# Weights staged through one tile: where the rounding is done, how many groups are in flight, and which engine forms the sums of weight blocks

## The chip, the cores and the metric

The kernel runs on one core of one Trainium2 chip. The time is device microseconds (us) from launch to end; the profile's span is the time from the first to the last instruction of one profiled execution. The engines are TensorE (PE), VectorE (DVE), ScalarE (ACT), GpSimd (POOL) and SyncE (SP, which here only issues DMAs). GpSimd issues DMAs too. Each engine runs its own instructions strictly in the order in which they were built.

## The reference, cut to what matters

A two-step attention (8 batches, 8 heads, 576 rows, 32 pack rows) feeds a gated layer and then a second layer. The weights arrive as float64.

```python
def _attn_ref(q, k, v, p):
    ...
    p_packed = sm_attn(p, k, v)
    out = sm_attn(q, p_packed, p_packed)
    return out.astype(np.float32)

def _moe_ref(x, w_gate, w_val, w_out):
    gate = 1.0 / (1.0 + np.exp(-(x @ w_gate)))
    val = x @ w_val
    return (gate * val @ w_out).astype(np.float32)

def _moe2_ref(x, w_in, w_out):
    h = x @ w_in
    g = np.maximum(0.01 * h, h)
    return (g @ w_out).astype(np.float32)
```

Shapes: x is 4608 x 512; w_gate and w_val are 512 x 1536, w_out of the first layer 1536 x 512, w_in 512 x 2048, w_out of the second layer 2048 x 512.

## The kernel before, in words

The program has two parts. In the **gated part** the attention of batch b+1 and the gated products of batch b run side by side. Each batch has 12 gate steps: a step is two products on TensorE (L692), a sigmoid on ScalarE (L702, so there are 96 of them in all), a multiplication on VectorE (L708) and a store of the result to DRAM (`g1d`). In the **block part** six blocks of 768 tokens go through the remaining three products (L852, 5544 matrix multiplications) with a seven-product scheme for 2x2 blocks of matrices. It needs sums and differences of blocks of the weights and of the data.

Weights are float64 in DRAM, so each 128 x 512 piece is loaded as pairs of 32-bit words (`raw64`) and rounded to float32 by a **unit** of five instructions: `scale` and `low` on ScalarE, `shift` and `sign` on VectorE, and the integer addition `total` on GpSimd, which writes the result. In the kernel before, the first four work in tiles of their own, `cvs` and `cvf`, three of each. The first 24 units give the gating weights (tiles `wc`, which stay). The other 44 units belong to 22 **staged groups**, two units each, for the weights of the block part. A group has a tile `Y` of eight 256-column slots. Its two units fill four slots, `combine` fills the four others with sums and differences (four instructions, in two pairs), and then each half of `Y` (four slots and three) is split in a high and a low part: `high` on ScalarE (L317) casts it into a tile `HL`, `low` on GpSimd (L323) subtracts, and a DMA issued by GpSimd (L331) stores `HL` in DRAM (`wp`, `wu`, `wd`). There are two tiles `Y` and two tiles `HL`.

The order of instructions is made when the program is built, by a small planner. It walks through modelled time, gives each engine the ready task of lowest rank, and counts the tiles of each pool. Staged groups have rank 900 and more, behind everything in the gated part (`high` and `low` of a group are lifted to rank -1100). The costs that the planner assumes are formulas such as `gps(n)` for GpSimd; what it assumes for a DMA is its size plus 2.2 us.

Between the parts stand two markers. `opened_left` comes after all stored groups and all units: then the pool `stage` (raw64, cvs, cvf, Y, HL) gives its place to the tiles `rawg` and `wu` of the block part, so no load of the block part can start earlier. `opened_right` comes after the last gate step: then the pool of the attention gives its place to the operands `op`, so the block part's casts cannot start earlier.

```python
        opened_left = add("", 0, 0, open_left, sum([*stored.values(), *units], []))
        opened_right = add("", 0, 0, open_right, [glu_end[B - 1]])
```

Of the kernel before, what the change touches and what calls it, by code (L numbers as in the profile page):

```python
# [10 lines left out]
F32 = mybir.dt.float32  # L11
F32R = mybir.dt.float32r
I32 = mybir.dt.int32
U32 = mybir.dt.uint32
AF = mybir.ActivationFunctionType
ALU = mybir.AluOpType
AX = mybir.AxisListType
P = 128
# [11 lines left out]
class Plan:  # L30
# [15 lines left out]
    def add(self, engine, us, rank, fn, after=(), take=(), give=()):  # L46
        i = len(self.tasks)
        self.tasks.append((engine, us, rank, fn, [a for a in after if a is not None], take, give))
        for name in dict.fromkeys(name for name, _ in take):
            self.pools[name][1].append(i)  # L50
        for key in give:
            self.holders[key] = self.holders.get(key, 0) + 1
        return i
# [66 lines left out]
def act(n):  # L120
    return 0.13 + n * 0.00094


def dve(n):
    return 0.15 + n * 0.00105


def gps(n):
    return 0.05 + n * 0.0027
# [3 lines left out]
def pack_attention_glu_lrelu(  # L133
# [22 lines left out]
    nc = tc.nc  # L156
# [39 lines left out]
    stage = tc.alloc_tile_pool(name="stage", bufs=1, side="left")  # L196
# [7 lines left out]
    add = plan.add  # L204
# [6 lines left out]

    for name, n in (("raw64", 4), ("cv", 3), ("Y", 2), ("HL", 2)):
        plan.pool(name, n)

    def unit(key, rank, load, target, after=(), give=(), loads=1):

        t = {}

        def do_load():
            t["raw"] = stage.tile([P, 512, 2], I32, tag="raw64", bufs=4, name="raw64")
            load(t["raw"])

        def scale():
            t["s"] = stage.tile([P, 512], F32, tag="cvs", bufs=3, name="cvs")
            t["f"] = stage.tile([P, 512], I32, tag="cvf", bufs=3, name="cvf")
            nc.scalar.activation(t["s"], t["raw"][:, :, 1].bitcast(F32), AF.Copy, scale=2.0 ** -112)

        def low():  # L230
            nc.scalar.activation(t["f"], t["raw"][:, :, 0].bitcast(U32), AF.Copy, scale=2.0 ** -29)

        def shift():
            s = t["s"].bitcast(I32)
            nc.vector.tensor_single_scalar(s, s, 3, op=ALU.logical_shift_left)  # L235

        def sign():
            s = t["s"].bitcast(I32)
            nc.vector.scalar_tensor_tensor(  # L239
                out=s, in0=t["raw"][:, :, 1], scalar=-(1 << 31), in1=s,  # L240
                op0=ALU.bitwise_and, op1=ALU.bitwise_or,
            )

        def total():
            x = target().bitcast(I32)
            n = x.shape[1]
            nc.gpsimd.tensor_tensor(  # L247
                out=x,
                in0=t["s"].bitcast(I32).rearrange("p (a b) -> p a b", a=n),
                in1=t["f"].rearrange("p (a b) -> p a b", a=n),  # L250
                op=ALU.add,
            )

        L = add("DMA", 1.7, rank, do_load, after, take=[("raw64", ("raw64", key))])
        a = add("ACT", act(512), rank, scale, [L], take=[("cv", ("cv", key))])
        c = add("ACT", act(512), rank, low, [a], give=[("raw64", key)])
        s = add("DVE", 0.42, rank, shift, [a])
        s = add("DVE", 0.75, rank, sign, [s], give=[("raw64", key)])
        return add("POOL", gps(512), rank, total, [c, s, *after], give=[("cv", key), *give])

    def unit_gv(i, g, jh):
        w = (w_gate, w_val)[g]
# [17 lines left out]
    def staged(st, g, kk, rank):  # L280

        key, t = (st, g, kk), {}
# [17 lines left out]
        def target(half):  # L300
            def fn():
                if "y" not in t:
                    t["y"] = stage.tile([P, 8, 256], F32, tag="Y", bufs=2, name="Y")
                return t["y"][:, 0:2] if half else t["y"][:, 6:8]
            return fn

        def combine(*ops):
            def fn():
                y = t["y"]
                for o, a, b, op in ops:  # L310
                    nc.vector.tensor_tensor(out=y[:, o], in0=y[:, a], in1=y[:, b], op=op)  # L311
            return fn

        def high(x0, x1):
# [22 lines left out]
        y = ("Y", key)  # L337
        begin = add("", 0, rank, lambda: None, take=[("Y", y)])
        us = [unit((key, half), rank + 0.1 * half, load(half), target(half), [begin]) for half in range(2)]
        a1 = add("DVE", 2 * dve(256), rank, combine((2, 7, 1, ALU.add), (3, 2, 6, ALU.subtract)), us)  # L340
        a2 = add("DVE", 2 * dve(256), rank, combine((4, 6, 7, ALU.subtract), (5, 0, 3, ALU.subtract)), [a1])
        stored[key] = []
        for a, x0, x1 in ((a1, 0, 4), (a2, 4, 7)):
            n = (x1 - x0) * 256
# [414 lines left out]
    def block(n, opened_left, opened_right):  # L759
# [75 lines left out]
        def products(st, gm, gs, u, made, keep, finish):  # L835
# [3 lines left out]
            def key(*x):  # L839
                return (*x, n, st, gm)  # L840
# [35 lines left out]
            for i in ORDER:  # L876
                c = CHAIN[i]
                for g in gs:
                    wg = gm if st == "u" else g
                    L = load_weights(st, wg, i, u)  # L880
                    begin, end = g == gs[0], g == gs[-1]
                    task = add(
                        "PE", 2.07, u, mm(i, g, ("wu", n, st, wg, i), begin, end),
                        [L, made[i, g], *wait.get(i, [])],
                        take=[("acc", key("acc", c))] if begin and i in (1, 5, 6) else [],
# [155 lines left out]
    with tc.manual_schedule():  # L1041
# [11 lines left out]
        rank = 900.0  # L1053
# [39 lines left out]
```

## Time and profile before

| | us |
|---|---|
| median of 3 runs (1563.97 to 1570.9) | 1567.53 |
| time of the profiled execution | 1571.51 |
| its span | 1569.7 |
| PE busy in the span | 1426.4 |
| DVE busy in the span | 1082.0 |
| ACT busy in the span | 768.0 |
| POOL busy in the span | 437.7 |

The busy times are sums over the whole span. PE is busy for 91% of it. The profiled execution lies 4.0 us above the median, and its time 1.8 us above its span.

### The profile page before, as it was taken

What the parts mean: (1) busy time and instruction counts of PE and PEld (TensorE: products, weight loads), DVE (VectorE), ACT (ScalarE), POOL (GpSimd) and SP (SyncE); (2) the same over time, 40 slices, a digit from 0 to 9 for tenths busy, and PEclk for the clock granted to TensorE, in tenths of its full rate; (3) what the DMA queues carried; (4) which work ended last, traced back from release to release, by engine and by line L of the source; (5) the groups of instructions that cost most, each with busy time, mean ns of one, the idle gap of its engine ahead of it and who ended that gap; (6) DMA issues with size and microseconds to landing.
All of it is one profiled execution on the core that took longest, in us unless ns stands there. A gap on an engine that the chain in (4) does not pass through costs nothing.

```text
span 1569.7 us, 26707 instructions
## 1 busy us (share of the span) xinstructions
PE 1426.4 (91%) x10368; PEld 1336.0 (85%) x10368; DVE 1082.0 (69%) x1438; ACT 768.0 (49%) x1017; POOL 437.7 (28%) x514
## 2 busy tenths in 40 slices
PE   4687989998889828999999999999999999999995
PEld 1565777876768718999999999999999999999995
DVE  5787878967877627668566865687558755885491
ACT  4476666756565524454345433554355434543450
POOL 1332343314345652001710160026001620130006
PEclk8898999999999959999999999999999999999998
DMA  9994686776566879888998899889988898898884
GB/s 227 255 249 153 224 302 221 251 248 213 189 232 228 293 272 355 295 253 264 324 331 254 261 336 320 252 263 319 334 253 264 288 364 257 256 290 253 253 255 120
DMA packets 143070, 414.92 MB, mean 264 GB/s; under 512 B 24544, under 2 KB 35552, under 8 KB 142944
## 3 DMA queue, kind: packets, MB, share of 16 engines
q1 hardware_dynamic: 115744, 335.07, 67.3%
q0 software_dynamic: 27200, 78.14, 14.5%
q8 instruction: 83, 1.36, 0.4%
q14 instruction: 43, 0.35, 0.1%
HBM read 335.02 MB, written 78.12 MB: 263 GB/s over the span
## 4 chain that ended last, share of the span: by engine, by line
PE 70%; DMA 12%; DVE 7%; ACT 4%; POOL 3%; issue 3%; SPq 0%; POOLq 0%; ACTq 0%; DVEq 0%
PE ps_pair L852 60%; PE ps_pair L692 8%; DMA wd<-HL 2%; DMA raw<-in_moe_w_gate_dram 2%; DMA raw<-in_moe_w_out_dram 2%; DMA wu<-HL 1%; DVE Y L311 1%; DMA v<-in_v_dram 1%; POOL out_dram L1027 1%; POOL HL L323 1%; DVE ml L676 1%; DMA rawg<-g1d 1%; PE ps_pair L659 1%; POOL Y L247 1%; DVE cvs L235 1%
## 5 line engine op out<-in xcount | busy, mean ns | idle before, releaser
L852 PE MATMUL ps_pair<-op,wu 128*128 128x384 f32 x5544 | 965.7, 337 | 39.5 <-DMA wu<-wp 33.5
L852 PEld LDWEIGHTS ps_pair<-op,wu 128*128 128x128 f32 x5544 | 963.6, 189 | 41.5 <-ACT op L795 33.5
L1027 POOL DMA_DIRECT2D out_dram<-os x256 | 150.3, 595 | 618.8 <-DVE os L1014 609.5
L795 ACT CAST op<-rawg 128x768 fp32r<-128x768 f32 x168 | 138.3, 835 | 245.3 <-DVE rawg L786 121.3
L692 PE MATMUL ps_pair<-Ah,ml 128*128 128x288 f32 x768 | 181.1, 318 | 52.8 <-DVE ml L676 22.5
L800 DVE TENSOR_TENSOR op<-rawg,op 128x768 fp32r<-128x768 f32 x168 | 158.3, 951 | 87.3 <-ACT op L795 86.1
L692 PEld LDWEIGHTS ps_pair<-Ah,ml 128*128 128x128 f32 x768 | 126.9, 197 | 101.9 <-ACT sg L702 27.6
L869 DVE TENSOR_TENSOR tmp<-ps_pair,tmp 128x768 f32<-128x768 f32 x72 | 68.8, 956 | 154.4 <-PE ps_pair L852 106.0
L692 PE MATMUL ps_pair<-Al,mh 128*128 128x288 f32 x768 | 169.9, 303 | 0.3 <-DVE Al L581 0.2
L692 PE MATMUL ps_pair<-Ah,mh 128*128 128x288 f32 x768 | 169.0, 302 | 0.0
L795 ACT CAST op<-G 128x768 fp32r<-128x768 f32 x168 | 134.7, 834 | 59.8 <-PE ps_pair L852 44.8
L800 DVE TENSOR_TENSOR op<-G,op 128x768 fp32r<-128x768 f32 x168 | 155.7, 948 | 7.7 <-ACT op L795 7.3
L323 POOL TENSOR_TENSOR HL<-Y,HL 128x1024 fp32r<-128x1024 f32 (+1 forms) x44 | 94.7, 2155 | 129.7 <-ACT HL L317 128.3
L692 PEld LDWEIGHTS ps_pair<-Al,mh 128*128 128x128 f32 x768 | 128.6, 196 | 0.9 <-DVE Al L581 0.9
L692 PEld LDWEIGHTS ps_pair<-Ah,mh 128*128 128x128 f32 x768 | 127.8, 195 | 0.0
L925 POOL DMA_DIRECT2D rawg<-g1d x96 | 68.0, 712 | 160.7 <-ACT op L795 66.6
L988 ACT ACTIVATE G<-G 128x768 f32<-128x768 f32 x96 | 81.2, 846 | 59.0 <-DVE G L985 58.0
L247 POOL TENSOR_TENSOR Y<-cvs,cvf 128x512 int32<-128x512 int32 x44 | 58.5, 1334 | 149.2 <-DVE cvs L239 104.8
L863 ACT COPY tmp<-ps_pair 128x768 f32<-128x768 f32 x72 | 57.5, 799 | 84.5 <-PE ps_pair L852 84.0
L786 DVE TENSOR_TENSOR rawg<-rawg 128x768 f32<-128x768 f32 x96 | 90.2, 952 | 4.1 <-DMA rawg<-g1d 3.3
L786 DVE TENSOR_TENSOR G<-G 128x768 f32<-128x768 f32 x96 | 91.1, 950 | 0.3
L708 DVE TENSOR_TENSOR sg<-sg,ps_pair 128x576 f32<-128x576 f32 x96 | 71.5, 744 | 28.0 <-ACT sg L702 11.2
(75 smaller groups left out, 1147.3 us busy)
## 6 DMA issues: line engine op xcount, KB each, us to landing
wu<-wu SPq DMA_DIRECT2D x168, 512.0 KB, 4.6
wu<-wd SPq DMA_DIRECT2D x168, 512.0 KB, 4.5
wu<-wp SPq DMA_DIRECT2D x126, 512.0 KB, 5.0
g1d<-sg SPq DMA_DIRECT2D x96, 288.0 KB, 4.0
rawg<-g1d POOLq DMA_DIRECT2D x48, 384.0 KB, 8.7
raw<-in_moe_w_out_dram SPq DMA_DIRECT2D x28, 512.0 KB, 6.8
raw<-in_k_dram SPq DMA_DIRECT2D x16, 576.0 KB, 5.1
raw<-in_q_dram SPq DMA_DIRECT2D x16, 576.0 KB, 6.2
```

What stands on the lines that cost most here:

```text
L247: nc.gpsimd.tensor_tensor(out=x, in0=t["s"].bitcast(I32).rearrange("p (a b) -> p a b", a=n), in1=t["f"].rearrange("p (a b) -> p a b", a=n) ...
L323: nc.gpsimd.tensor_tensor(out=hl[:, :, 1], in0=t["y"][:, x0:x1], in1=hl[:, :, 0].bitcast(F32), op=ALU.subtract,)
L692: nc.tensor.matmul(ps[:, t, :HS], w, x[:, t * HS:(t + 1) * HS], start=(n == 0), stop=(n == len(pairs) - 1),)
L708: nc.vector.tensor_tensor(out=sg, in0=sg, in1=st["gv", f, 1][:, :, :HS], op=ALU.mult)
L786: nc.vector.tensor_tensor(out=src(g, o), in0=src(g, a), in1=src(g, b), op=ALU.subtract)
L795: nc.scalar.copy(h, src(g, c))
L800: (nc.gpsimd if on_pool(i, g) else nc.vector).tensor_tensor(out=l, in0=src(g, c), in1=tiles["op", st, i, g][0].bitcast(F32), op=ALU.subtract)
L852: nc.tensor.matmul(ps[c][:, m, :TB], a, x[:, kk, :], start=(fresh and kk == 0 and y == 0), stop=(end and kk == 1 and y == 2), skip_group_c ...
L869: nc.vector.tensor_tensor(out=T[x], in0=ps[c][:, :, :TB], in1=T[y], op=ALU.add)
L925: nc.gpsimd.dma_start(out=t[:, :, t0 - base:t0 - base + m], in_=g1d[b][:, f:f + 2, s0:s0 + m])
L988: nc.scalar.activation(dest(), dest(), AF.Prelu, alpha=0.01)
L1027: nc.gpsimd.dma_start(out=ob[:, s0:s0 + m, d0:d0 + 32], in_=tiles["os", c][32 * y:32 * y + 32, x, t0:t0 + m],)
```

## The change: what it does

1. `scale` writes its float32 result into the tile of the result at once (`wc` or a slot pair of `Y`); `shift`, `sign` and `total` work there in place. The tile `cvs` is gone; the pool `cv` counts only `cvf` and is taken at `low`. So it is now `scale` that waits for a free `Y`, and the load of `raw64` no longer does. Into `wc`, the rows written are two runs of 256 columns instead of one of 512.
2. There are three tiles `Y` instead of two.
3. The four sums and differences of a group go from VectorE to GpSimd (88 instructions of 128 x 256 in all).
4. The planner is told new costs: 0.6 and 0.78 us for `shift` and `sign`, and GpSimd's formula for the sums.

```diff
-    for name, n in (("raw64", 4), ("cv", 3), ("Y", 2), ("HL", 2)):
+    for name, n in (("raw64", 4), ("cv", 3), ("Y", 3), ("HL", 2)):
...
         def scale():
-            t["s"] = stage.tile([P, 512], F32, tag="cvs", bufs=3, name="cvs")
-            t["f"] = stage.tile([P, 512], I32, tag="cvf", bufs=3, name="cvf")
-            nc.scalar.activation(t["s"], t["raw"][:, :, 1].bitcast(F32), AF.Copy, scale=2.0 ** -112)
+            x = t["x"] = target()
+            nc.scalar.activation(
+                x, t["raw"][:, :, 1].bitcast(F32).rearrange("p (a b) -> p a b", a=x.shape[1]),
+                AF.Copy, scale=2.0 ** -112,
+            )
...
         def total():
-            x = target().bitcast(I32)
-            n = x.shape[1]
+            x = t["x"].bitcast(I32)
             nc.gpsimd.tensor_tensor(
-                out=x,
-                in0=t["s"].bitcast(I32).rearrange("p (a b) -> p a b", a=n),
-                in1=t["f"].rearrange("p (a b) -> p a b", a=n),
-                op=ALU.add,
+                out=x, in0=x, in1=t["f"].rearrange("p (a b) -> p a b", a=x.shape[1]), op=ALU.add
             )
 
-        L = add("DMA", 1.7, rank, do_load, after, take=[("raw64", ("raw64", key))])
-        a = add("ACT", act(512), rank, scale, [L], take=[("cv", ("cv", key))])
-        c = add("ACT", act(512), rank, low, [a], give=[("raw64", key)])
-        s = add("DVE", 0.42, rank, shift, [a])
-        s = add("DVE", 0.75, rank, sign, [s], give=[("raw64", key)])
-        return add("POOL", gps(512), rank, total, [c, s, *after], give=[("cv", key), *give])
+        L = add("DMA", 1.7, rank, do_load, take=[("raw64", ("raw64", key))])
+        a = add("ACT", act(512), rank, scale, [L, *after])
+        c = add("ACT", act(512), rank, low, [a], take=[("cv", ("cv", key))], give=[("raw64", key)])
+        s = add("DVE", 0.6, rank, shift, [a])
+        s = add("DVE", 0.78, rank, sign, [s], give=[("raw64", key)])
+        return add("POOL", gps(512), rank, total, [c, s], give=[("cv", key), *give])
...
-                    t["y"] = stage.tile([P, 8, 256], F32, tag="Y", bufs=2, name="Y")
+                    t["y"] = stage.tile([P, 8, 256], F32, tag="Y", bufs=3, name="Y")
...
-                    nc.vector.tensor_tensor(out=y[:, o], in0=y[:, a], in1=y[:, b], op=op)
+                    nc.gpsimd.tensor_tensor(out=y[:, o], in0=y[:, a], in1=y[:, b], op=op)
...
-        a1 = add("DVE", 2 * dve(256), rank, combine((2, 7, 1, ALU.add), (3, 2, 6, ALU.subtract)), us)
-        a2 = add("DVE", 2 * dve(256), rank, combine((4, 6, 7, ALU.subtract), (5, 0, 3, ALU.subtract)), [a1])
+        a1 = add("POOL", 2 * gps(256), rank, combine((2, 7, 1, ALU.add), (3, 2, 6, ALU.subtract)), us)
+        a2 = add("POOL", 2 * gps(256), rank, combine((4, 6, 7, ALU.subtract), (5, 0, 3, ALU.subtract)), [a1])
```

How the planner now orders the instructions shows at three places. The changed file is shorter by one line there, so L317 of before is L316 of the changed kernel, L702 is L701, L795 is L794, L713 is L712.

**ScalarE, end of the gated part.** `sg` rows are the sigmoids of gate steps, `HL` rows the casts of the staged groups, `cvs` and `cvf` rows belong to units, and `op` rows are the first casts of the block part. Before:

```order
L702 ACTIVATE sg<-ps_pair 128x576 x2
L317 CAST HL<-Y 128x4x256
L317 CAST HL<-Y 128x3x256
L228 ACTIVATE cvs<-raw_6287 128x512
L231 ACTIVATE cvf<-raw_6287 128x512
L228 ACTIVATE cvs<-raw_6298 128x512
L231 ACTIVATE cvf<-raw_6298 128x512
L317 CAST HL<-Y 128x4x256
L317 CAST HL<-Y 128x3x256
L795 CAST op<-rawg 128x768 x11
```

Changed, at the last cast into `HL`:

```order
L701 ACTIVATE sg<-ps_pair 128x576
L316 CAST HL<-Y 128x3x256
L672 CAST mh<-ps_pair 128x1024
L316 CAST HL<-Y 128x4x256
L701 ACTIVATE sg<-ps_pair 128x576
L316 CAST HL<-Y 128x3x256
```

Changed, at the end of the gated part:

```order
L701 ACTIVATE sg<-ps_pair 128x576 x2
L672 CAST mh<-ps_pair 128x1024
L701 ACTIVATE sg<-ps_pair 128x576 x3
L794 CAST op<-rawg 128x768 x5
L862 COPY tmp<-ps_pair 128x768
L794 CAST op<-rawg 128x768 x4
```

Before, two groups end behind the last sigmoid (the 96th); in the changed order the last cast of the last group stands behind the 78th, and nothing of the staging stands between the last sigmoid and the block part. Of the 44 casts into `HL`, those that stand behind fewer than 12 sigmoids, 12 to 23, 24 to 35 and so on are 0, 5, 5, 6, 4, 6, 7, 7 and 4 (behind the 96th) before, and 2, 6, 10, 4, 8, 8, 6, 0 and 0 in the changed order.

**GpSimd, the last staged group.** `Y<-cvs,cvf` and `Y<-Y,cvf` are `total`, `HL<-Y,HL` is `low`, `Y<-Y` the sums, `wd_75` the store, and `rawg` the first loads of the block part. Before:

```order
L331 DMA wd_75<-HL 128x4x512
L247 TENSOR_TENSOR Y<-cvs,cvf 128x512
L331 DMA wd_75<-HL 128x3x512
L247 TENSOR_TENSOR Y<-cvs,cvf 128x512
L323 TENSOR_TENSOR HL<-Y,HL 128x4x256
L323 TENSOR_TENSOR HL<-Y,HL 128x3x256
L331 DMA wd_75<-HL 128x4x512
L331 DMA wd_75<-HL 128x3x512
L925 DMA rawg<-g1d_57 128x2x384 x3
```

Changed:

```order
L322 TENSOR_TENSOR HL<-Y,HL 128x4x256
L249 TENSOR_TENSOR Y<-Y,cvf 128x512
L330 DMA wd_75<-HL 128x4x512
L310 TENSOR_TENSOR Y<-Y 128x256 x2
L322 TENSOR_TENSOR HL<-Y,HL 128x3x256
L310 TENSOR_TENSOR Y<-Y 128x256 x2
L330 DMA wd_75<-HL 128x3x512
L322 TENSOR_TENSOR HL<-Y,HL 128x4x256
L330 DMA wd_75<-HL 128x4x512
L322 TENSOR_TENSOR HL<-Y,HL 128x3x256
L330 DMA wd_75<-HL 128x3x512
L924 DMA rawg<-g1d_57 128x2x384 x3
```

The sums now stand in GpSimd's own queue, in pairs, between the additions, the subtractions and the stores of neighbouring groups.

**SyncE, the first loads of staged weights.** `wu` rows are those loads, `g1d_63` and `g1d_64` rows the stores of gate steps of the last two batches, `raw` rows the loads of float64 pieces. Before:

```order
L713 DMA g1d_64<-sg 128x576 x3
L288 DMA raw_6287<-in_moe_w_out_dram 128x1024
L713 DMA g1d_64<-sg 128x576
L288 DMA raw_6298<-in_moe_w_out_dram 128x1024
L767 DMA wu<-wp_65 128x1024
L767 DMA wu<-wp_66 128x1024
```

Changed:

```order
L712 DMA g1d_62<-sg 128x576 x2
L712 DMA g1d_63<-sg 128x576 x10
L766 DMA wu<-wp_65 128x1024
L712 DMA g1d_63<-sg 128x576
L766 DMA wu<-wp_66 128x1024
L712 DMA g1d_63<-sg 128x576
L766 DMA wu<-wp_67 128x1024
```

The first loads of staged weights moved from behind the last load of a float64 piece to a place among the last stores of batch 6, a batch earlier; all six that there is room for stand ahead of the last ten stores of the last batch.

## Rows read from the trace of the kernel before

**Rows 1.** The page: span, and the chain that ended last, by engine.

```profile
span 1569.7 us, 26707 instructions
...
PE 70%; DMA 12%; DVE 7%; ACT 4%; POOL 3%; issue 3%; SPq 0%; POOLq 0%; ACTq 0%; DVEq 0%
```

**Rows 2.** Busy time by stretch: between the parts, and block part (us and instructions).

```profile
546.91:613.29 66.38, 27.30 (x145) 26.28 (x145) 34.27 (x41) 25.05 (x33) 30.01 (x33) 0.74 0.82 298
613.29:1543.78 930.49, 930.10 (x5354) 929.34 (x5355) 622.73 (x697) 409.45 (x509) 183.31 (x298) 1.00 0.88 286
```

**Rows 3.** Timeline, 546 to 581 us: start, duration, engine, what [idle before].

```profile
546.48 0.43 PE L692 MATMUL ps_pair<-Ah,mh 128*128 128x288 f32 x2
...
547.01 0.75 DVE L708 TENSOR_TENSOR sg<-sg,ps_pair 128x576 f32<-128x576 f32 x1 [0.30 <-issue]
...
565.42 1.53 POOL L331 DMA_DIRECT2D wd<-HL  x2
572.69 5.65 POOL L925 DMA_DIRECT2D rawg<-g1d  x8 [5.74 <-issue]
...
579.28 0.83 ACT L795 CAST op<-rawg 128x768 fp32r<-128x768 f32 x1 [16.77 <-DMA rawg<-g1d]
...
580.14 0.96 DVE L800 TENSOR_TENSOR op<-rawg,op 128x768 fp32r<-128x768 f32 x1 [19.30 <-ACT op L795]
...
580.16 0.69 PE L852 MATMUL ps_pair<-op,wu 128*128 128x384 f32 x1 [33.25 <-DMA wu<-wp]
```

**Rows 4.** Busy time between every twelfth sigmoid: PE, PEld, DVE, ACT, POOL, clock, DMA.

```profile
122.76:189.05 66.29, 55.53 (x587) 46.04 (x587) 55.17 (x94) 40.42 (x56) 17.06 (x12) 0.92 0.63 209
189.05:251.81 62.76, 56.68 (x592) 45.98 (x593) 50.73 (x81) 39.23 (x57) 25.03 (x18) 0.92 0.75 253
251.81:310.33 58.52, 57.26 (x677) 46.50 (x677) 52.24 (x96) 42.88 (x61) 24.32 (x17) 1.00 0.71 237
310.33:367.38 57.05, 52.53 (x533) 43.12 (x532) 43.70 (x68) 30.73 (x44) 17.61 (x13) 0.97 0.66 211
367.38:432.26 64.88, 57.34 (x611) 47.19 (x618) 51.95 (x82) 40.06 (x57) 24.17 (x18) 0.95 0.69 226
432.26:500.58 68.32, 61.22 (x655) 50.91 (x654) 48.35 (x81) 43.21 (x60) 29.69 (x22) 0.95 0.65 227
500.58:545.36 44.78, 40.76 (x320) 35.20 (x320) 32.04 (x45) 25.54 (x38) 30.01 (x23) 0.96 0.81 289
sum 422.60, PE 381.32 PEld 314.94 DVE 334.18 ACT 262.06 POOL 167.90; mean PE 54.47 PEld 44.99 DVE 47.74 ACT 37.44 POOL 23.99
```

**Rows 5.** Instructions of four lines: duration in ns, least, median and most.

```profile
L311 DVE TENSOR_TENSOR Y<-Y x88: 381/424/2610, 132.1 to 560.4; 128x256 f32<-128x256 f32 x88
...
L235 DVE TENSOR_SCALAR cvs<-cvs x68: 378/421/1619, 11.9 to 555.7; 128x512 int32<-128x512 int32 x68
...
L247 POOL TENSOR_TENSOR Y<-cvs,cvf x44: 1264/1288/1625, 106.0 to 558.0; 128x512 int32<-128x512 int32 x44
```

**Rows 6.** What ScalarE waited for ahead of L317: us in all, times.

```profile
  DVE Y L311: 31.0, 17
```

**Rows 7.** Timeline of GpSimd, first and last of five first halves in the tail.

```profile
496.70 2.40 POOL L323 TENSOR_TENSOR HL<-Y,HL 128x1024 fp32r<-128x1024 f32 x1 [4.69 <-ACT HL L317]
...
547.56 2.33 POOL L323 TENSOR_TENSOR HL<-Y,HL 128x1024 fp32r<-128x1024 f32 x1 [1.74 <-ACT HL L317]
552.96 1.82 POOL L323 TENSOR_TENSOR HL<-Y,HL 128x768 fp32r<-128x768 f32 x1 [3.07 <-ACT HL L317]
```

**Rows 8.** Timeline of GpSimd and VectorE around 189 us, side by side.

```profile
189.22 2.38 POOL L323 TENSOR_TENSOR HL<-Y,HL 128x1024 fp32r<-128x1024 f32 x1 [1.94 <-ACT HL L317]
...
189.73 2.48 DVE L311 TENSOR_TENSOR Y<-Y 128x256 f32<-128x256 f32 x2
```

**Rows 9.** Groups of instructions: busy us, mean ns of one, and idle before.

```profile
L311 DVE TENSOR_TENSOR Y<-Y 128x256 f32<-128x256 f32 x88 | 56.0, 666 | 9.5 <-POOL Y L247 8.6
...
L235 DVE TENSOR_SCALAR cvs<-cvs 128x512 int32<-128x512 int32 x68 | 42.8, 639 | 27.8 <-ACT cvs L228 27.7
```

More of the change, by code (lines that the diff above doesn't have):

```diff
@@ L225, in scale, with low @@
         def scale():
-            t["s"] = stage.tile([P, 512], F32, tag="cvs", bufs=3, name="cvs")
+            x = t["x"] = target()
[3 more added lines that the diff above has]
+            )
+        def low():
             t["f"] = stage.tile([P, 512], I32, tag="cvf", bufs=3, name="cvf")
-            nc.scalar.activation(t["s"], t["raw"][:, :, 1].bitcast(F32), AF.Copy, scale=2.0 ** -112)
@@ L230, in low @@
-        def low():
             nc.scalar.activation(t["f"], t["raw"][:, :, 0].bitcast(U32), AF.Copy, scale=2.0 ** -29)
         def shift():
-            s = t["s"].bitcast(I32)
-            nc.vector.tensor_single_scalar(s, s, 3, op=ALU.logical_shift_left)
+            x = t["x"].bitcast(I32)
+            nc.vector.tensor_single_scalar(x, x, 3, op=ALU.logical_shift_left)
         def sign():
-            s = t["s"].bitcast(I32)
+            x = t["x"].bitcast(I32)
             nc.vector.scalar_tensor_tensor(
-                out=s, in0=t["raw"][:, :, 1], scalar=-(1 << 31), in1=s,
-                op0=ALU.bitwise_and, op1=ALU.bitwise_or,
+                out=x, in0=t["raw"][:, :, 1].rearrange("p (a b) -> p a b", a=x.shape[1]),
+                scalar=-(1 << 31), in1=x, op0=ALU.bitwise_and, op1=ALU.bitwise_or,
@@ L242, in sign @@
             )
         def total():
-            x = target().bitcast(I32)
-            n = x.shape[1]
+            x = t["x"].bitcast(I32)
             nc.gpsimd.tensor_tensor(
-                out=x,
-                in0=t["s"].bitcast(I32).rearrange("p (a b) -> p a b", a=n),
-                in1=t["f"].rearrange("p (a b) -> p a b", a=n),
-                op=ALU.add,
-            )
-        L = add("DMA", 1.7, rank, do_load, after, take=[("raw64", ("raw64", key))])
-        a = add("ACT", act(512), rank, scale, [L], take=[("cv", ("cv", key))])
```

## The prediction

> **What bounds the kernel now.** I read the chain that ended last first: TensorE has 70% of it, and the rest is DMA, VectorE and ScalarE work that must lie where TensorE waits [rows 1]. So the second view is busy time by stretch. In the block part TensorE is busy for 930.10 of 930.49 us at full clock [rows 2]; nothing that the change touches is in that stretch, and it can become neither shorter nor longer. Between the last gated matrix multiplication, which ends at 546.91 us, and 613.29 us TensorE does only 27.30 us of work, at a granted clock of 0.74 [rows 2, 3]. The reader should see there that this hole isn't the price of changing parts as such. The timeline names its cause: the last multiplication of a gate step ends at 547.8 us, but GpSimd issues the last two stores of staged weights from 565.42 us on, the first load of the block part goes out at 572.69 us, and ScalarE's first cast waits for it until 579.28 us [rows 3]. The last staged groups are late, not the gated part.
>
> How large is the hole in terms of the block part? In 930.10 us it runs 5354 recorded multiplications, 0.1737 us each; the 145 that lie before 613.29 us would need 25 us [rows 2]. So the block part runs as if it had started, undisturbed, at 613.3 - 25.0 = 588.3 us. From 546.9 us that makes 41.4 us lost.
>
> The gated part is the third view, cut at every twelfth sigmoid [rows 4]. Over seven such stretches TensorE is busy for 381.3 of 422.6 us: 41.3 us are idle, spread thin. VectorE is busy for 50 us of an average 63 in the first six, GpSimd for 23.
>
> **The change, part by part.**
>
> *Moving the staging ahead.* By the order of the changed kernel the last cast of the last group stands behind the 78th sigmoid, where two groups stood behind the 96th. Engines are in order, so the staging must be over about 18 gate steps before the gated part is. A gate step took 44.78/12 = 3.7 us where no attention ran beside it [rows 4], so the six loads of staged weights and those of `rawg` have more than 50 us where they now have none. What is left of the hole is the hand-over that needs the last gate step: its multiplication ends 0.9 us after TensorE, one cast of 0.83 us and one subtraction of 0.96 us follow [rows 3], together about 3 us. Then comes a start-up, in which casts, subtractions and differences of the first operands must keep ahead of TensorE. In the run of before TensorE lost 33.1 - 25.0 = 8.1 us between 580.16 and 613.29 us, with the loads late as well [rows 2, 3]. With the loads done, the start-up is between nothing and 8 us; I take 4, the middle. Gain: 41.4 - 3 - 4 = 34 us.
>
> *The sums on GpSimd.* The trace has no floating-point addition of 256 columns on GpSimd. The nearest rows are its additions of 512 columns, 1.288 us in the median [rows 5], and subtractions of 1024 and 768 columns, 2.40 and 1.82 us [rows 7]. The last two give 2.27 ns for a column and so 0.66 us for 256; half of 1.288 is 0.64, and going down from 1.288 by 2.27 ns a column gives 0.71. I take 0.70 us, 2.8 us for a group and 62 us for all 88. GpSimd's work for a group becomes 2 x 1.29 + 2.8 + 2.40 + 1.82 + two DMA issues of 0.77 (1.53 for two [rows 3]) = 11.1 us. VectorE is rid of 56.0 us [rows 9]; only 88 x 0.424 = 37 us of these are the work itself [rows 5], the rest is waiting, to which I come.
>
> *How fast can a group be staged?* In the tail, where nothing but two tiles `HL` holds the staging, four periods take 547.56 - 496.70 = 50.9 us, 12.7 us a group [rows 7]. If the sums take 2.8 us there for VectorE's 4 x 0.424 = 1.7, the period is 13.8 us; if all of the 2.8 us came on top, 15.5. Between the tenth and the 78th sigmoid there are 68 steps, and at the 63 us that twelve steps take [rows 4] that is 357 us. Twenty-two groups need 304 us at 13.8 and 341 at 15.5. So it fits on the whole, but not everywhere: ten casts, five groups, stand in the 24th to 35th step, and 5 x 13.8 = 69 us is 6 more than the 62.8 us that this stretch took [rows 4]. The stretches with four groups need 55 us of 57.1 and 64.9, which fits. At 15.5 us a group the same count gives 15 + 5 = 20 us. Since a cast that waits holds up the sigmoids behind it in ScalarE's queue, this lengthens the gated part, by 6 us as I take it (the sums replace VectorE's rather than come on top), by 20 at most.
>
> *What is gained beside it.* ScalarE waited 31.0 us, 17 times, for VectorE's sums [rows 6]; those waits now depend on GpSimd instead. If they and VectorE's relief gave back a third of the 41.3 us of idle time in the gated part, it would be 15 us shorter. I take nothing of it, because the casts still wait for sums and stores, and keep 15 as the bound.
>
> *Rounding in place, and the third tile.* `scale`, `low`, `sign` and `total` keep their element counts; ScalarE, VectorE and GpSimd write as much as before. `shift` could take longer where its rows are two runs: a median of 0.421 us now [rows 5], and if it cost the 0.639 that it has on average [rows 9], 68 x 0.22 = 15 us of VectorE's time lie beside a VectorE that the sums leave with 37 us less. At no cost on the path; the cover is VectorE's idle 13 us in each stretch of 63 [rows 4].
>
> *Sum.* The profiled execution took 1571.5 us. Less 34, plus 6: 1543.5. It lies 4.0 us above the median of the runs, so against the median the same sum is 1567.5 - 28 = 1539.5. I say 1539.
>
> **What speaks against it: the port of GpSimd and VectorE.** An instruction of VectorE on two operands in SBUF can be held up by GpSimd: at 189.22 us GpSimd starts a subtraction of 2.38 us, and two sums that VectorE starts at 189.73 take 2.48 us for two where the median is 0.42 each [rows 5, 8]. The worst single sum took 2610 ns [rows 5]. In the mean a sum lost 0.666 - 0.424 = 0.24 us and a shift 0.22 [rows 5, 9], while GpSimd was busy for a third of the time. The sums leave VectorE, and with them this loss of 21 us, but GpSimd will be busy about twice as much, and shifts, signs and the softmax's subtractions and products stay on VectorE: some twenty in a stretch of 63 us (four in each of three or four groups, six of the attention). At twice the loss, 0.45 us each, that is 9 us of a VectorE which had 13 idle and lost 8 of work: no term.
>
> The Trainium skill, in "SBUF — State Buffer", section "Who interferes with whom", has this as an exclusive lock: a VectorE instruction with two SBUF inputs and a GpSimd instruction that reads SBUF exclude each other, and whichever is second is blocked for the whole of the other. By that rule a held-up instruction waits for what is left of an addition or subtraction, half of 1.3 to 2.4 us on average; the rows at 189 us agree with it. The sum would be the same by either, but the rule bears out the slower rival below, in which the waits are long ones.
>
> **The rivals.**
> 1. *GpSimd becomes the bound of the staging* and its waits move into the gated part: the period is 15.5 us, the gated part 20 us longer, 1567.5 - 34 + 20 = 1553.5. For it: 11.1 us of 12.7 are GpSimd's own work. Against it: the planner spaced the casts with GpSimd at 1.43 us for an addition that takes 1.29 (its formula, 0.05 + 512 x 0.0027), so it left GpSimd room.
> 2. *The gated part gets shorter too*, by 15 us, with VectorE relieved: 1567.5 - 34 - 15 = 1518.5. For it: VectorE is the busiest engine there after TensorE. Against it: TensorE's idle pieces are short and stretches with few groups idle no less.
> 3. *VectorE waits for GpSimd at every two-operand instruction* (the other side). Without the sums of three groups (12 x 0.666 us = 8) VectorE needs about 42 us of 63; twenty instructions that wait w each add 20w. It becomes the bound at w = 1.0 us, and at w = 1.3 six stretches longer by 5 us each, 30 in all, eat the gain of 28: from there on the kernel is slower. At w = 1.5 it takes 1567.5 - 34 + 6 x 9 = 1587. Against it: w is 0.22 now.
> 4. *The hole stays in another shape*: the block part's first operands wait for a load or for space that is freed as late as before, and the 34 us shrink to what the gated part loses. 1567. Against it: both markers and all loads stand earlier in the order; only `opened_right` hangs on the last gate step.
>
> **How the numbers follow.** My forecast gets 0.52, rival 1 0.18, rival 2 0.14, rival 3 0.08, rival 4 0.08. The likeliest case's own range is 1528 to 1550 (6 us either way for the stretch of ten casts, 4 for the start-up). The range runs from rival 2 to past rival 1, 1518 to 1560; rivals 3 and 4 lie outside. A measurement of this kernel can tell about 0.5%, 8 us. Forecast, rival 1 and rival 2 are all faster by more: 0.84. Rival 4 is the same, 0.08; rival 3 slower, 0.08.
>
> **What the changed profile should show.** The last store of staged weights is issued some 60 us before the last gated multiplication; the first cast into `op` begins within 2 us of the last multiplication of a gate step, and TensorE's wait at the change of parts is about 3 us, not 33. The block part's 930 us stand. A sum on GpSimd takes 0.65 to 0.75 us and GpSimd is busy for some 62 us more. The stretch from the 24th to the 36th sigmoid is the one that grows. I am wrong if the last gated multiplication ends later than 567 us (rival 1 and beyond), if shifts take over 1 us in the median (rival 3), or if the first operands wait for DMA (rival 4).

## The result and the profile after

The changed kernel takes 1539.96 us in the median of four runs (1537.68 to 1542.83), the kernel before beside it 1568.99. The ratio is 0.9822 with a 95% interval of 0.9802 to 0.9842 (the quotient of these two medians alone would be 0.9815). The forecast was 1539 us.

The page, span and the chain that ended last:

```profile
span 1535.9 us, 26671 instructions
...
PE 78%; DMA 8%; DVE 5%; ACT 4%; issue 2%; POOL 2%; SPq 1%; POOLq 0%; ACTq 0%; DVEq 0%
```

TensorE's share of the chain went from 70% to 78% [rows 1]. The second view is busy time by stretch: from the end of the gated part to 615 us, and on to the last sum but one of the block part, which began at 1543.78 us in the kernel before. The columns are those of [rows 2].

```profile
549.39:615.00 65.61, 61.06 (x337) 60.28 (x337) 46.50 (x53) 28.48 (x37) 8.66 (x12) 0.95 0.79 277
615.00:1509.96 894.96, 894.96 (x5164) 894.70 (x5163) 602.09 (x674) 399.89 (x497) 178.67 (x290) 1.00 0.87 284
```

Before, 66.4 us behind the gated part held 27.3 us of TensorE's work [rows 2]; now 65.6 us hold 61.1. From the end of the gated part to that sum it was 66.4 + 930.5 = 996.9 us, and it is 960.6: the hole gave 36.3 us. The gated part itself ends 2.5 us later (549.4 us for 546.9). 36.3 - 2.5 = 33.8 is the whole difference of the two spans. The medians differ by 29.0 only: the profiled execution of before lies 2.5 us above its median here, that of the changed kernel 2.3 below. So no sum of terms from this one pair is good to better than 5 us.

The timeline around the change of parts, GpSimd first, then VectorE, ScalarE and TensorE:

```profile
484.95 0.77 POOL L330 DMA_DIRECT2D wd<-HL  x1 [0.30 <-POOL HL L322]
489.70 7.20 POOL L924 DMA_DIRECT2D rawg<-g1d  x10 [3.98 <-DMA wd<-HL]
...
549.48 0.76 DVE L707 TENSOR_TENSOR sg<-sg,ps_pair 128x576 f32<-128x576 f32 x1 [2.42 <-PE ps_pair L691]
...
552.50 3.76 ACT L794 CAST op<-rawg 128x768 fp32r<-128x768 f32 x5 [4.01 <-DMA g1d<-sg]
...
553.39 0.69 PE L851 MATMUL ps_pair<-op,wu 128*128 128x384 f32 x1 [4.00 <-ACT op L794]
```

The last staged store is issued 64 us ahead of the last gated multiplication, the loads of the block part follow 4 us later, when that store has landed, and TensorE waits 4.00 us instead of 33.25 [rows 3]. What is left isn't only cast and subtraction: the first cast waits until the last gate step's store has landed (`DMA g1d<-sg`), 2.3 us after that step's multiplication on VectorE, because `op` takes over the memory of the pool that holds `sg`.

The gated part, cut at every twelfth sigmoid:

```profile
124.22:194.03 69.81, 54.44 (x583) 44.94 (x591) 57.53 (x92) 45.43 (x64) 38.56 (x34) 0.90 0.80 262
194.03:257.39 63.36, 57.09 (x659) 46.49 (x666) 51.44 (x74) 42.02 (x58) 50.96 (x44) 0.97 0.85 280
257.39:321.50 64.11, 57.70 (x638) 47.64 (x619) 53.62 (x88) 46.95 (x70) 32.41 (x28) 0.97 0.82 265
...
444.38:503.66 59.28, 55.10 (x605) 44.72 (x604) 42.68 (x61) 35.35 (x48) 48.47 (x50) 0.97 0.67 238
503.66:547.84 44.18, 44.18 (x370) 39.16 (x369) 16.08 (x19) 12.88 (x18) 0.28 (x1) 1.00 0.50 189
sum 423.62, PE 377.84 PEld 313.91 DVE 324.55 ACT 264.10 POOL 257.21; mean PE 53.98 PEld 44.84 DVE 46.36 ACT 37.73 POOL 36.74
```

GpSimd's work in these stretches rose from 167.9 to 257.2 us, and the whole is 1 us longer [rows 4]. The last stretch has no staging and no idle TensorE.

The lines that answer to the sums and shifts of before (duration in ns: least, median, most):

```profile
L310 POOL TENSOR_TENSOR Y<-Y x88: 720/742/1293, 111.3 to 476.4; 128x256 f32<-128x256 f32 x88
...
L238 DVE TENSOR_SCALAR Y<-Y x44: 377/896/3843, 105.6 to 450.4; 128x512 int32<-128x512 int32 x44
...
L242 DVE SCALAR_TENSOR_TENSOR Y<-raw,Y x44: 650/886/2485, 107.4 to 452.4; 128x512 int32<-128x512 int32 x44
```

A sum takes 0.742 us. A shift of a staged unit takes twice what shifts took (0.421) [rows 5]. That hangs on the order of this kernel and not on the edits as such: kernel 5 below has the same rounding, the same sums on GpSimd and three `Y`, and its median is 0.426.

### The profile page after: what moved, and what is told of

It reads as the page before. It is cut to its first block, busy times and chain, and to the rows that moved or that the text cites. A ratio compares the mean times of both kernels' runs of the same rounds, so it can differ in the third digit from the quotient of the medians.

```text
span 1535.9 us, 26671 instructions
## 1 busy us (share of the span) xinstructions
PE 1422.4 (93%) x10368; PEld 1335.8 (87%) x10368; DVE 1067.9 (70%) x1350; ACT 763.8 (50%) x1015; POOL 510.0 (33%) x602
## 4 chain that ended last, share of the span: by engine, by line
PE 78%; DMA 8%; DVE 5%; ACT 4%; issue 2%; POOL 2%; SPq 1%; POOLq 0%; ACTq 0%; DVEq 0%
PE ps_pair L851 62%; PE ps_pair L691 13%; PE ps_pair L658 2%; DMA raw<-in_moe_w_gate_dram 2%; DMA raw<-in_moe_w_val_dram 2%; POOL out_dram L1026 1%; DMA wd<-HL 1%; DVE ml L675 1%; DVE Y L238 1%; PE ps_pair L427 1%; DMA raw<-in_moe_w_in_dram 1%; DMA wu<-wu 1%; DVE Y L242 1%; ACT mh L672 1%; ACT L701 1%
## 5 line engine op out<-in xcount | busy, mean ns | idle before, releaser
L794 ACT CAST op<-rawg 128x768 fp32r<-128x768 f32 x168 | 137.7, 835 | 211.8 <-DVE rawg L785 104.4
L794 ACT CAST op<-G 128x768 fp32r<-128x768 f32 x168 | 134.6, 834 | 59.8 <-PE ps_pair L851 44.8
L701 ACT ACTIVATE sg<-ps_pair 128x576 f32<-128x576 f32 x96 | 62.4, 650 | 82.5 <-PE ps_pair L691 77.3
```

The costliest lines, as they stand in the source:

```text
L701: nc.scalar.activation(st["sg", f], st["gv", f, 0][:, :, :HS], AF.Sigmoid)
L794: nc.scalar.copy(h, src(g, c))
```

## The experiments

Twelve kernels were run. In the table, the second column is read from each kernel's order; the next three are from its profiled execution (end of the gated part, TensorE's wait at the change of parts, time); median and ratio are of all its runs, the ratio against runs of the kernel before taken beside them. A profiled execution can lie up to 7 us off the median of its kernel, so ends of gated parts can be compared no closer than that.

| kernel | last cast behind sigmoid | gated part ends | wait | profiled | median | ratio [95%] |
|---|---|---|---|---|---|---|
| before | 96 | 546.9 | 33.3 | 1571.5 | 1569.0 | |
| changed | 78 | 549.4 | 4.0 | 1537.7 | 1540.0 | 0.9822 [0.9802, 0.9842] |
| 1 early load alone | 82 | 552.2 | 4.0 | 1543.4 | 1541.8 | 0.9829 [0.9806, 0.9852] |
| 2 sums alone | 96 | 526.5 | 58.8 | 1574.5 | 1578.8 | 1.0062 [1.0043, 1.0081] |
| 3 sums back on VectorE | 79 | 570.3 | 4.0 | 1558.2 | 1556.7 | 0.9926 [0.9911, 0.9941] |
| 4 two Y | 80 | 545.0 | 4.0 | 1531.9 | 1537.5 | 0.9805 [0.9772, 0.9838] |
| 5 late load, three Y | 86 | 549.1 | 5.9 | 1538.1 | 1538.4 | 0.9805 [0.9786, 0.9825] |
| 6 late load, two Y | 96 | 523.5 | 65.7 | 1579.2 | 1579.4 | 1.0064 [1.0047, 1.0082] |
| 7 early load and sums | 77 | 558.1 | 4.0 | 1545.1 | 1539.4 | 0.9813 [0.9788, 0.9837] |
| 8 two Y, sums on VectorE | 87 | 546.1 | 6.3 | 1536.5 | 1543.3 | 0.9838 [0.9817, 0.9860] |
| 9 staging last | behind all | 493.8 | 277.0 | 1760.7 | 1760.7 | 1.1231 [1.1207, 1.1255] |
| 10 sums twice | 77 | 568.7 | 4.0 | 1556.1 | 1557.3 | 0.9941 [0.9918, 0.9963] |
| 11 three HL, two Y | 77 | 558.9 | 4.0 | 1547.6 | 1542.9 | 0.9847 [0.9825, 0.9869] |
| 12 planner's landing time | 78 | 542.6 | 4.0 | 1531.4 | 1530.4 | 0.9762 [0.9743, 0.9782] |

**1. The early load alone.** A side effect of rounding in place is that the load of a piece no longer waits for a free `Y`. Here it is the only edit of the kernel before:

```diff
-        L = add("DMA", 1.7, rank, do_load, after, take=[("raw64", ("raw64", key))])
+        L = add("DMA", 1.7, rank, do_load, take=[("raw64", ("raw64", key))])
```

> The kernel before with one edit: the load of a float64 piece no longer waits for a free Y. Own tiles for the rounding, two Y and sums on VectorE stay. In its order the last cast into HL stands behind the 82nd sigmoid (96 before, 78 in the changed kernel). Theory A (the time follows from where the staging ends, and the early load is what moves it): the hole at the change of parts shrinks from 33 us of waiting to about 4, 1535 to 1550 us. Theory B (it is the relief of VectorE by the moved sums): 1560 us or more, since VectorE keeps the sums. Theory C (it is the third Y): no change, 1568 us.

1541.8 us, by the ratios within 0.1% of the changed kernel. Theory A holds here; B and C fall. First TensorE instruction of the block part:

```profile
556.19 0.69 PE L852 MATMUL ps_pair<-op,wu 128*128 128x384 f32 x1 [4.00 <-ACT op L795]
```

**2. The sums alone.** The kernel before with the sums on GpSimd:

```diff
-                    nc.vector.tensor_tensor(out=y[:, o], in0=y[:, a], in1=y[:, b], op=op)
+                    nc.gpsimd.tensor_tensor(out=y[:, o], in0=y[:, a], in1=y[:, b], op=op)
...
-        a1 = add("DVE", 2 * dve(256), rank, combine((2, 7, 1, ALU.add), (3, 2, 6, ALU.subtract)), us)
+        a1 = add("POOL", 2 * gps(256), rank, combine((2, 7, 1, ALU.add), (3, 2, 6, ALU.subtract)), us)
...
```

> The kernel before with the sums on GpSimd and nothing else. In its order eight casts, four groups, stand behind the last sigmoid, where four casts stood. Theory A: the tail of the staging gets longer by up to two groups at 12.7 us, less the two groups that no longer lie in the gated part; 1570 to 1595 us. Theory B: a gain of its own from a shorter gated part, 1540 to 1555 us. Theory C: 1568 us.

1578.8 us, 0.6% slower, as theory A had it. The first multiplication of the block part:

```profile
585.28 0.69 PE L852 MATMUL ps_pair<-op,wu 128*128 128x384 f32 x1 [58.80 <-DMA rawg<-g1d]
```

The gated part ends 20 us earlier, which theory B had claimed, but the wait behind it is 25.6 us longer than before, because the planner leaves four groups behind the last sigmoid.

**3. The sums back on VectorE**, all else as changed (the edit of 2 in reverse).

> The changed kernel with the sums back on VectorE (rounding in place and three Y stay). Last cast behind the 79th sigmoid. Theory A: hole closed as in the changed kernel, 1535 to 1548 us, the same as the changed kernel within 0.5%. Theory B: the gated part is longer by VectorE's 56 us spread over it, at least 10 us more than the changed kernel: 1550 us or more. Theory C: 1540 us.

1556.7 us, 17 us more than the changed kernel: here theory A missed, and the time lies in B's range. The hole is closed as expected (4.0 us), so all of it is in the gated part, 21 us longer.

**4. Two Y**, all else as changed:

```diff
-    for name, n in (("raw64", 4), ("cv", 3), ("Y", 3), ("HL", 2)):
+    for name, n in (("raw64", 4), ("cv", 3), ("Y", 2), ("HL", 2)):
...
-                    t["y"] = stage.tile([P, 8, 256], F32, tag="Y", bufs=3, name="Y")
+                    t["y"] = stage.tile([P, 8, 256], F32, tag="Y", bufs=2, name="Y")
```

> The changed kernel with two Y instead of three (rounding in place and sums on GpSimd stay). Last cast behind the 80th sigmoid. Theory A: 1536 to 1548 us, the third Y buys nothing that can be measured. Theory B: 1540 us too. Theory C (third Y): back to 1560 us or more.

1537.5 us, the same. With the early load, the third `Y` buys nothing that can be measured.

**5 and 6. The late load, with three and with two Y.** The changed kernel with the one condition put back (6 has the edit of 4 as well):

```diff
-        L = add("DMA", 1.7, rank, do_load, take=[("raw64", ("raw64", key))])
+        L = add("DMA", 1.7, rank, do_load, after, take=[("raw64", ("raw64", key))])
```

> The changed kernel with one part undone: the load of a float64 piece waits for a free Y again, as before. Three Y, rounding in place and sums on GpSimd stay. In its order the last cast into HL stands behind the 86th sigmoid (78 in the changed kernel). Theory A1 (early load and third Y are two ways to the same thing, either is enough): ten gate steps of 3.7 us still lie behind the staging, the hole stays closed, 1535 to 1550 us. Theory A2 (the early load alone does it): the hole comes back, 1560 us or more.

> The same with two Y: rounding in place and sums on GpSimd, but the load waits for a free Y and there are two of them. Eight casts, four groups, stand behind the last sigmoid. Theories A1 and A2: the hole is back and longer than before, as with the sums alone, 1570 to 1590 us. Rival (rounding in place with sums on GpSimd is itself the gain): 1545 us or less.

1538.4 us with three `Y`, 1579.4 us with two. Theory A1 holds. Either the early load or the third `Y` is enough, and without both the hole is back, twice as long as before (65.7 us for 33.3, with four groups behind the last sigmoid instead of two), though rounding in place and sums on GpSimd are still there. The third `Y` was run only together with these two, never on the kernel before alone. First multiplication of the block part in kernel 6:

```profile
589.21 0.69 PE L851 MATMUL ps_pair<-op,wu 128*128 128x384 f32 x1 [65.72 <-DMA wu<-wp]
```

**7. Early load and sums**, that is the edits of 1 and 2 together, on the kernel before.

> The kernel before with the early load and with the sums on GpSimd; own tiles for the rounding, two Y, the old costs. Last cast behind the 77th sigmoid. If the sums on GpSimd shorten the gated part by 20 us whatever else stands there, as the run with the sums alone and the run with the sums back on VectorE both suggest: 1515 to 1528 us, faster than the changed kernel. If the short gated part of the run with the sums alone only came from the four groups that lay behind it: 1535 to 1545 us, the same as the changed kernel.

1539.4 us, 2 us less than with the early load alone, within the intervals. Its gated part ends at 558.1 us, so the short gated parts of 2 and 6 came from the four groups that lay behind them, not from the sums. This pair also shows what the move is worth to VectorE: kernels 1 and 7 differ in it alone, and VectorE's busy time over the whole span falls by 36.3 us. From the page of each, first 1, then 7:

```profile
PE 1421.9 (92%) x10368; PEld 1331.0 (86%) x10368; DVE 1106.9 (72%) x1438; ACT 760.8 (49%) x1013; POOL 439.8 (29%) x514
```

```profile
PE 1425.5 (92%) x10368; PEld 1335.6 (87%) x10368; DVE 1070.6 (69%) x1350; ACT 768.9 (50%) x1019; POOL 513.1 (33%) x602
```

**8. Two Y, sums on VectorE**: rounding in place and early load are left of the change (edits of 3 and 4).

> The changed kernel with the sums on VectorE and two Y: rounding in place, early load and new costs are left. Last cast behind the 87th sigmoid, nine steps or 33 us ahead of the end, so the hole should be closed. It tells why the run with the sums back on VectorE and three Y had a gated part 18 us longer than the run with the early load alone. If rounding in place is what costs there: 1550 to 1562 us. If it is the third Y (more groups at a time in a gated part whose VectorE is full): 1538 to 1548 us.

1543.3 us, in the range given to the third `Y`. Rounding in place costs nothing that shows (1 has 1541.8). What makes kernel 3 slow is the third `Y` together with sums on VectorE; with the early load, each without the other is harmless.

**9. Staging last.** Every group is held back until the last gate step:

```diff
-        begin = add("", 0, rank, lambda: None, take=[("Y", y)])
+        begin = add("", 0, rank, lambda: None, [glu_end[B - 1]], take=[("Y", y)])
```

> The changed kernel with every staged group held back until the last gate step, so that the gated part runs with none of them. It is meant for two numbers, not for its time: where the gated part ends without any staging, and how long 22 groups take with all engines to themselves. If a group costs the gated part 6 us (the two kernels with 18 groups ahead of the last sigmoid end their gated part near 525 us, those with 22 near 549), it ends near 420 us. If the gated part is bound by its own work for most of that, it ends at 490 us or later. The staging itself: 22 groups at 12.7 to 15.5 us, 280 to 340 us; in all 1740 to 1880 us.

The gated part without staging ends at 493.8 us, near the second guess. Busy time behind it and in it:

```profile
494.00:763.00 269.00, 0.00 (x0) 0.00 (x0) 178.99 (x89) 91.70 (x130) 251.24 (x220) 0.50 0.66 229
120.00:492.00 372.00, 366.05 (x3980) 304.67 (x3979) 230.93 (x384) 185.66 (x250) 0.00 (x0) 0.99 0.37 116
```

Without staging TensorE is busy for 366 of 372 us: the gated part is bound by TensorE. In the changed kernel it ends 549.4 - 493.8 = 55.6 us later, so a staged group costs it 2.5 us in the mean. The cost isn't even: with 18 groups ahead of the last sigmoid (kernels 2 and 6) the gated part ends at 526.5 and 523.5 us, 1.7 to 1.8 us a group, and the last four of the changed kernel cost some 6 each. Some 12 us of the 55.6 are TensorE's own work taking longer: 377.84 us in the seven stretches above, at granted clocks of 0.90 to 1.00, for 366.05 here, at 0.99. Most of the rest is idle time.

Alone, 22 groups take 269 us, less than the 280 to 340 expected, 12.2 each, and GpSimd is busy for 251 of these, 93%: by itself the staging is bound by GpSimd.

**10. Every sum twice**, with the planner told of it (the second time changes no value):

```diff
-                for o, a, b, op in ops:
+                for o, a, b, op in ops + ops:
...
-        a1 = add("POOL", 2 * gps(256), rank, combine((2, 7, 1, ALU.add), (3, 2, 6, ALU.subtract)), us)
+        a1 = add("POOL", 4 * gps(256), rank, combine((2, 7, 1, ALU.add), (3, 2, 6, ALU.subtract)), us)
...
```

> The changed kernel with every sum done twice on GpSimd, the planner told of it: 88 more instructions of 0.74 us, 65 us in all, 14.3 us of GpSimd's work for a group instead of 11.3. Last cast behind the 77th sigmoid. If GpSimd has room and the sums lie beside other work: within 6 us of the changed kernel, 1537 to 1546 us. If GpSimd is what the gated part waits for (rival 1 of the prediction): 1555 us or more.

1557.3 us, 17 us more: the time of rival 1. Between the twelfth and the 84th sigmoid, first the changed kernel, then this one:

```profile
124.22:503.66 379.44, 333.66 (x3592) 274.75 (x3593) 308.47 (x450) 251.22 (x352) 256.93 (x228) 0.95 0.81 268
```

```profile
121.13:520.65 399.52, 341.08 (x3600) 274.90 (x3593) 336.42 (x450) 253.85 (x356) 324.88 (x309) 0.94 0.74 253
```

GpSimd got 68 us more to do. VectorE runs the same 450 instructions in both, and they take 28 us longer. The mechanism isn't that of rival 1, though. ScalarE's casts into `HL` wait no longer than before (42.3 us in all for 41.2). What grew is the time that TensorE waits for VectorE, from 18.6 to 35.4 us; for ScalarE it waits 22.7 us instead of 27.8. The longest of these waits (us, times, longest), changed kernel first:

```profile
PE ps_pair L691 <- DVE ml L675: 7.4, 6, 2.8
PE ps_pair L503 <- DVE ml L675: 4.3, 1, 4.3
```

```profile
PE ps_pair L691 <- DVE ml L675: 13.6, 8, 4.0
PE ps_pair L427 <- DVE ml L675: 9.2, 2, 6.3
```

That is the price of more work on GpSimd: VectorE stands still beside it, and TensorE waits for VectorE.

**11. Three HL, two Y.**

```diff
-    for name, n in (("raw64", 4), ("cv", 3), ("Y", 3), ("HL", 2)):
+    for name, n in (("raw64", 4), ("cv", 3), ("Y", 2), ("HL", 3)):
...
-                    t["y"] = stage.tile([P, 8, 256], F32, tag="Y", bufs=3, name="Y")
+                    t["y"] = stage.tile([P, 8, 256], F32, tag="Y", bufs=2, name="Y")
...
-                hl = t[x0] = stage.tile([P, 4, 2, 256], F32R, tag="HL", bufs=2, name="HL")
+                hl = t[x0] = stage.tile([P, 4, 2, 256], F32R, tag="HL", bufs=3, name="HL")
```

> The changed kernel with two Y and three HL, in place of three Y and two HL. ScalarE's casts waited 36 us for stores of HL in the changed kernel. If these waits cost the gated part: 1520 to 1532 us, faster than the changed kernel. If they only delay the staging, which has time: the same, 1534 to 1544 us.

1542.9 us, the same. What ScalarE's casts into `HL` wait for (us, times), in the changed kernel and in this one:

```profile
  DMA wd<-HL: 14.8, 4
  DMA wp<-HL: 14.3, 4
  DMA wu<-HL: 7.1, 5
  POOL Y L310: 5.0, 4
```

```profile
  POOL Y L310: 17.7, 15
  DMA wp<-HL: 1.8, 1
```

The waits for stores went (36.2 to 1.8 us), those for the sums grew (5.0 to 17.7), and in all the casts wait half as long (19.5 for 41.2). Beside kernel 4, which lacks only the third `HL`, it is 19.5 for 50.8. The time didn't follow.

**12. The planner's landing time.**

```diff
-    LAG = {"DMA": 2.2}
+    LAG = {"DMA": 3.5}
```

> The changed kernel with one number of the planner changed: it counts 3.5 us instead of 2.2 for a DMA to land, so that casts stand later behind the stores they wait for (a store of HL of 1024 columns is then counted at 6.5 us; the trace has 5.6 in the median). If ScalarE's waits for stores cost the gated part: 1522 to 1534 us. If not: within 5 us of the changed kernel.

1530.4 us, 0.9762 of before; its interval lies clear of the changed kernel's. It is the fastest of all, some 9 us faster than the changed kernel. The casts into `HL` wait 20.7 us for stores instead of 36.2, and the gated part ends 7 us earlier in the profiled execution. That these waits cost the gated part is not shown by it alone, since kernel 11 has still fewer and gains nothing; the new order differs in other places too.

## Why the prediction was right, and where it was not

**The hole.** The prediction read 41.4 us of loss behind the gated part and kept 7 of it. By the same rule the changed kernel keeps 7.2: at the pace of its own block part (894.96/5164 = 0.1733 us) its 337 multiplications need 58.4 of the 65.6 us. 4.0 us of these are the hand-over, where 3 were counted, because of the store of the last gate step; 3.2 are the start-up, where 4 were taken. That 36.3 us were gained and not 34 lies in the kernel before, whose hole was undersized: at this pace its 5499 multiplications need 953 of the 996.9 us, so some 44 were lost. Its slow start goes on behind 613.29 us, where the prediction took the block part to run at full clock from the first. The kernel before, in the first 32 us behind that mark, had a granted clock of 0.95:

```profile
613.29:645.00 31.71, 31.71 (x174) 31.71 (x175) 17.85 (x20) 8.79 (x11) 5.02 (x8) 0.95 0.92 319
```

The mechanism is shown both ways: each kernel whose order ends the staging behind the 77th to 87th sigmoid waits 4 to 6.3 us there, and those with two or four groups behind the 96th wait 33 to 66 (kernel 9, with all of them there, 277). One sign of being wrong was met to the letter: the first cast does wait for a DMA, the store of the last gate step, and begins 2.3 us behind that step's multiplication where "within 2 us" was said. It costs 1 us and isn't the hole of rival 4.

**How near the number came.** 1539 for 1540 is in part luck. The terms were -34 and +6, a gain of 28; the profiled pair has -36.3 and +2.5, a gain of 33.8. The medians show 29.0, nearer to the forecast, since the two profiled executions lie on opposite sides of their medians.

**What moves the staging.** The prediction took the whole move from the order of the changed kernel and did not ask which edit made it. Kernels 1, 4, 5 and 6 answer: the load that no longer waits for `Y`, or a third `Y`, either one. In both cases a group's loads can start while the groups ahead still hold their tiles. The sums on GpSimd, the part with the most instructions, do not move it, and alone they make the kernel slower (2).

**The sums.** 0.70 us was estimated, 0.742 is the median, but the mean is 0.831 (71.9 us for 88, where 62 were counted). Some last up to 1.29 us, so sums can be delayed on GpSimd too:

```profile
L310 POOL TENSOR_TENSOR Y<-Y 128x256 f32<-128x256 f32 x88 | 71.9, 831 | 2.3
```

**The gated part.** +6 us were forecast, +2.5 measured in the one pair of profiles. The sum is near, the place is wrong, so the sum is luck. The stretch from the 24th to the 36th sigmoid, which was to grow by 6, grew by 0.6; the one before grew by 3.5 and the one after by 5.6, and the stretch from the 72nd to the 84th lost 9.0 [rows 4]. The step that failed is the one from a dense stretch of casts to a longer gated part, by casts that wait and hold up the sigmoids behind them: kernel 11 halves the waits of the casts and gains nothing, and in kernel 10 the gated part grows by 19 us with these waits unchanged.

The period of a group was sized at 13.8 us from a tail in which the prediction saw only the two `HL` at work. With the sums on GpSimd and no gated part beside it, it is 12.2 (kernel 9). There GpSimd works for 11.4 us of each 12.2, near the 11.1 that the prediction counted, while the casts still wait for `HL` (66.5 us in all). So for the staging by itself the nearer bound was GpSimd's own work.

**No term for VectorE.** The prediction let the relief of VectorE and the new waits at the port cancel: 9 us of waits against 8 of work in a stretch. In sum that came out nearly so: VectorE lost 88 instructions that took 56.0 us [rows 9], and its busy time went only from 1082.0 to 1067.9 us. But two parts of the change are mixed in this. The early load alone raises it to 1106.9 us (kernel 1), and in the four pairs of kernels whose only edit is the move of the sums (before and 2, 1 and 7, 3 and changed, 8 and 4) it falls by 32 to 46 us. The relief is real, but it buys time that can be told from noise in only one of these pairs (3 and changed, 17 us).

The 0.45 us for a held-up instruction was near: shifts of staged units take 0.58 us more than an undisturbed 0.421 in the mean, signs 0.33 more than 0.69. What lengthens a shift isn't its two runs of columns: in the gating weights, where it now has them, the median is 0.427 us before and after.

**The rivals.** Rival 3's bound of 1.0 us was not reached, yet kernel 10, which only adds to GpSimd, shows how it begins. Rival 1's time needs more of GpSimd's work than the changed kernel has, and kernel 10, which reaches it, does so through VectorE. Rival 2 fell: TensorE's idle time in the seven stretches is 423.6 - 377.8 = 45.8 us for 41.3. (Its bound was also misreckoned: a third of 41.3 us is 14, not 15.) Rival 4 is refuted by the 4.0 us.

**Left open.** Why a third `Y` with sums on VectorE costs 13 us (3 against 8) was not settled. Over the same 72 gate steps VectorE's busy time is alike in both, and TensorE idles more (55.6 us for 44.7), first 3, then 8:

```profile
126.54:522.33 395.79, 340.23 (x3592) 275.60 (x3593) 339.10 (x533) 259.19 (x358) 186.93 (x138) 0.94 0.77 256
```

```profile
122.90:506.71 383.81, 339.07 (x3656) 277.27 (x3657) 341.01 (x531) 258.46 (x358) 168.24 (x119) 0.97 0.75 251
```

It is the third `Y` by the comparison of kernels. Nearly all of the added idle time is spent waiting for VectorE (29.6 us for 18.8; for ScalarE 26.7 and 25.8), most of it at one copy that the attention needs, again 3 and then 8:

```profile
PE ps_pair L519 <- DVE pk L515: 13.2, 6, 3.8
```

```profile
PE ps_pair L519 <- DVE pk L515: 4.8, 4, 2.2
```

So VectorE is as busy but comes to that copy later. Which of the instructions ahead of it in the order cause this isn't shown; kernel 3 also has more of GpSimd's work in these steps (186.9 us for 168.2).

## What to carry to other kernels

Ask of a change with several parts which of them moves the critical work, and try the smallest alone: here one removed wait of a load, a by-product of another part, did what the whole change did. When background work ends behind the foreground work that hides it, where its last piece stands in the order counts more than how fast each piece is. Moving elementwise work from VectorE to GpSimd freed VectorE of 32 to 46 us and in three pairs of four bought no time that can be told from noise, and doubling that work on GpSimd cost 17 us, because VectorE then stood still beside it. A wait that can be removed isn't yet a wait that costs: halving those of the casts gained nothing.

## What the runs showed of the hardware

A VectorE instruction can be held up through several GpSimd instructions in a row, not only one, and it needs no two operands in SBUF for that: the shift here reads one tile. In the changed kernel, GpSimd and VectorE side by side:

```profile
326.93 1.30 POOL L249 TENSOR_TENSOR Y<-Y,cvf 128x512 int32<-128x512 int32 x1
328.15 0.77 POOL L330 DMA_DIRECT2D wu<-HL  x1
328.94 1.27 POOL L249 TENSOR_TENSOR Y<-Y,cvf 128x512 int32<-128x512 int32 x1
...
326.67 3.84 DVE L238 TENSOR_SCALAR Y<-Y 128x512 int32<-128x512 int32 x1
```

A shift that takes 0.42 us undisturbed lasts from 326.67 to 330.51 us, beside an addition, a DMA issue and a second addition of GpSimd, and ends 0.3 us after the latter. With staging alone (kernel 9) the 89 VectorE instructions behind the gated part took 179 us, 2.0 each, and single signs up to 9.3 us:

```profile
L242 DVE SCALAR_TENSOR_TENSOR Y<-raw,Y x44: 677/1208/9305, 495.2 to 728.9; 128x512 int32<-128x512 int32 x44
```

The Trainium skill, in "SBUF — State Buffer", section "Who interferes with whom", has the loser blocked for the whole of the other's instruction. The traces agree that it is blocked. They add that this can repeat: no single instruction of GpSimd takes more than 2.86 us in the changed kernel and 2.35 us in kernel 9, so the 3.4 us lost by the shift and the 8.6 us lost by the longest sign each span more than one.
